# Mirrored positions and 64x64 quadrants in the Fourier part of a fused S4 and PEER kernel

## The chip, the cores and the metric

The kernel runs on one core of one Trainium2 chip. The metric is the device time of one execution in microseconds; three runs of the kernel before gave a median of 1520.82 us (1519.2 to 1524.14).

## The reference

Two branches read the same input `u` (2048 positions, 576 channels) and are mixed by a gate.

```python
# branch A: a long convolution over positions, one kernel K per channel
P = jnp.exp(logdA[:, :, None] * l[None, None, :])
K = jnp.einsum("dn,dnl,dn->dl", Cc, P, dB).real
Kf, Uf = rfft(pad(K)), rfft(pad(u))
y = irfft(Uf * Kf)[:L] + u * Dskip
# branch B: PEER, per token and head the best 2 of 64 x 64 experts by two score tables
s1 = jnp.einsum("nhd,ed->nhe", q1, k1); s2 = jnp.einsum("nhd,ed->nhe", q2, k2)
# top_s, top_e: the best 2 of the 2 x 2 candidates of the two top-2 lists
g = softmax(top_s)
act = gelu(jnp.einsum("nd,nhkd->nhk", x, u[top_e]))
b = jnp.einsum("nhk,nhk,nhkd->nd", g, act, v[top_e])
# mix
gate = sigmoid((x * gate_w).sum(-1))
return gate * a + (1 - gate) * b
```

## The kernel before, in words

Five engines work on one program whose order was fixed when it was written out: Python generators (one per piece of work) run on a model of the engines' clocks, `pump` lets those go on whose inputs the model holds to be ready, and so their instructions come to stand between others. `mm` (line 202 in the profile holds every matmul) and the `Engine` wrapper (line 122: every DVE, ACT and POOL operation) keep that clock; `dma` (line 193) issues nearly all transfers on SP's queue. `quota`, `need`, `take` and `free` count PSUM banks (`sc` for scores, activations and outputs, `wb` for the rest) and buffers.

**PEER.** 128 groups of score matmuls (`s`, 14 matmuls 128x128x512 in fp16, one group per 8 score tables and 128 tokens), each followed on DVE by eight MAX8 and eight FIND_INDEX8 (`scores_top`). 128 groups of activation matmuls (`a`, 14 matmuls as well: all 4096 experts against all tokens), whose results go to DRAM by way of `go`. The main loop (lines 1495 to 1533) takes a group of the one or the other kind and calls `pump` between its matmuls. The list `acts` (line 1437) holds the order of the activation groups; its last 20 are those of expert block 7 with block 6's last one between. The output loop (line 1543) takes 16 tiles of 128 tokens: `prep(t)` loads the activations of tile t, builds one-hot matrices on DVE, scatters the gate weights by matmul (`S`), multiplies and splits them (`wh`), and 192 matmuls 128x128x288 (`o`) sum over the experts.

**The convolution.** The length-2048 transform is split into 32 x 64: stage 1 transforms over the 32 positions l1 of one residue l2 (64 residues), stage 2 over the 64 residues.
- `k_gen` makes K: 36 chunks of 16 channels, in fp32 matmuls 128x32x64 (`kb`); `k_store` splits a chunk into two fp16 parts in `ko` (two buffers) and stores it to `k_d`.
- `u_stage1` and `k_stage1` multiply by constant tables (`tu`, `tk`; fp16 in two parts) and store to `su_d` and `sk_d`, rows of residue, part (real, imaginary) and frequency k1. `k_stage1` has, for each of 32 pairs of residues, eight matmuls of 144 columns.
- `products` (line 1014): for each of 16 values of k and each third of the channels (192 columns), one fp32 product with the 128x128 matrix `f2` for u (`pu`) and one for K (`pk`), both with 2 x 192 columns. The matrix is the complex 64-point transform written out in real and imaginary parts. ACT copies the results into four tiles (`vf`, `ux`, `kr`, `kx`) such that real parts and imaginary parts stand where the complex multiplication wants them; POOL does two multiplications and an addition; the product with `fi` (`pv`) transforms back. It is sent out by `back` together with the forward products of three steps later. `store` copies it to `vo` and `z_d`.
- `y_part` does the inverse of stage 1, two output tiles at a time: fp32 products 128x64x288 with `tf` (`y`), scaled and added to `u * Dskip`. It runs inside the output loop: `load` asks for the next pair's data when the last pair is finished.

The stages follow one another in `freq`: load `ksb` (all of `k_d`), `k_stage1`, `products`, then the values' preparation and `prep(0)`.

Of the kernel before, what the change touches and what calls it, by code (L numbers as in the profile page):

```python
# [35 lines left out]
L2_POS = list(range(32)) + [63 - i for i in range(32)]  # L36
KB = 4
# [5 lines left out]
def _tables():  # L43
# [7 lines left out]
    def stacked(rows, inner):  # L51

        x = np.zeros((len(rows), 2, R1, 2, R1, 2))
        for b in range(2):
            x[:, b, :, b] = fwd[rows[:, b]]
        if inner:
            x = x.transpose(0, 1, 2, 5, 4, 3)
        else:
            x = x.transpose(0, 2, 1, 3, 5, 4)
        x = (x * 2.0 ** 14).reshape(len(rows), 64, 128)  # L60
        hi = x.astype(np.float16)
        lo = (x - hi).astype(np.float16)
        x = np.stack([np.concatenate([hi, hi], 1), np.concatenate([lo, np.zeros_like(lo)], 1)], 2)
        return np.ascontiguousarray(x.transpose(1, 0, 2, 3))

    tu = stacked(np.arange(R2).reshape(32, 2), False)
    tk = stacked(np.array(L2_POS)[:, None].repeat(2, 1), True)
    tf = np.zeros((NT, 2, 2, R1, 2, 2, R1))
    for t in range(NT):
        for pr in range(2):  # L70
            for b in range(2):
                w = 4 * t + 2 * pr + b
                tf[t, pr, b, :, :, b] = inv[w].transpose(1, 2, 0)
    tf = tf.transpose(0, 1, 2, 4, 3, 5, 6).reshape(NT * 2, 128, 64).transpose(1, 0, 2)
    k2 = np.arange(R2)
    al = 2 * np.pi * (np.outer(l2, k2) % R2) / R2
    c, s = np.cos(al), np.sin(al)
    f2 = np.zeros((R2, 2, 2, R2))
    f2[:, 0, 0], f2[:, 1, 0] = c, s
    f2[:, 0, 1], f2[:, 1, 1] = -s, c  # L80
    fi = np.zeros((2, R2, R2, 2))
    fi[0, :, :, 0], fi[1, :, :, 0] = c.T, -s.T
    fi[0, :, :, 1], fi[1, :, :, 1] = s.T, c.T
# [43 lines left out]
def body(ctx: ExitStack, tc: tile.TileContext, xT, au, par, logdt, dskip, gatew, wq, kT, uT, vv,  # L127
# [148 lines left out]
    quota(sc=4, wb=0, kb=4, hw=1, slot=9, go=3, m8=2, raw=1, ko=2)  # L276
# [8 lines left out]
    su_d = dr.tile([R2, 2, R1, D], F32, name="su_d")  # L285
    sk_d = dr.tile([R2, 2, R1, D], F32, name="sk_d")
    k_d = dr.tile([NCK, 128, 2, R2 * NI], F16, name="k_d")
    z_d = dr.tile([R2, 2, R1, D], F32, name="z_d")
# [12 lines left out]
    def au_load(a, t):  # L301
        for d, o in au_rows(au, t, a):
            dma(o, d)

# [467 lines left out]

    def k_store(c, kb):
# [5 lines left out]
        kz = ko.rearrange("p z (q i) -> p z q i", i=NI)  # L779
# [7 lines left out]
        kstored[0] += 1  # L787
# [135 lines left out]
    def u_stage1():  # L923
# [7 lines left out]
        def half(m):  # L931
            for n in range(m, 2 * NT, 2):
                a, o = us[:, m, :], us[:, 2 + m, :]
                for z in range(2):
                    dma(a[64 * z:64 * z + 64], bass.AP(tensor=au.tensor, offset=au.offset + 2 * n * D,
                                                       ap=[[64 * D, R1], [D, 2], [1, D]]))
# [8 lines left out]
                for hh in range(2):  # L945
# [6 lines left out]
                    ov = o.rearrange("p (b j q) -> p j b q", b=2, j=2)[:, hh]  # L952
                    S.activation(ov, pb[:, :288].rearrange("p (b q) -> p b q", b=2), AF.Copy)
# [3 lines left out]
                dma(su_d[2 * n:2 * n + 2].rearrange("b r k d -> (b r k) d"), o)  # L957
# [14 lines left out]
    def k_stage1(ksb, fk):  # L972
        enter, leave, count = ring(3)

        def tail(w, o, pbs):
            yield from ready(*pbs)
            for z in range(2):
                copy(o[:, z if w < 32 else 1 - z, :], pbs[z][:, :288])
                free("wb", o)
            yield from ready(o)  # L980
            l0 = min(L2_POS[w], L2_POS[w + 1])
            dma(bass.AP(tensor=sk_d.tensor, offset=sk_d.offset + l0 * R1 * 2 * D,
                        ap=[[288, 128], [R1 * 2 * D, 2], [1, 288]]), o)
# [7 lines left out]
        nxt = load(0)  # L991
        for w0 in range(0, 64, 16):
            tkt = nxt
            if w0 < 48:
                nxt = load(w0 + 16)
            yield from ready(tkt, ksb)
            for w in range(w0, w0 + 16, 2):
                yield from enter()
                o = fk.tile([128, 2, 288], F32, tag="s1o", name=f"k1o{w}", bufs=4)
                pbs = []  # L1000
                yield from need("wb", 2)
                for z in range(2):
                    pb = bank("wb", f"k1_{w}_{z}")
                    for jp in range(2):
                        for n in range(2):
                            mm(pb[:, 144 * jp:144 * jp + 144], tkt[:, w + z - w0, n], ksb[:, jp, :, w + z, :],
                               n == 0, n == 1)
                    pbs.append(pb)
                spawn(tail(w, o, pbs))
                del pb, pbs  # L1010
# [3 lines left out]
    def products(ff):  # L1014
# [11 lines left out]
        top, low = slice(0, 64), slice(64, 128)  # L1026
        made = []

        def tail(nm, pu, pk, v):

            t = lambda g: ff.tile([128, 2, PW], F32, tag=g, name=g + nm, bufs=2)
            ux, kr, ki = t("ux"), t("kr"), t("kx")
            two = lambda x: x[:, 0:2 * PW].rearrange("p (z q) -> p z q", z=2)
            yield from ready(pu)
            S.activation(v, two(pu), AF.Copy)
            S.activation(ux[top], two(pu)[low], AF.Copy)
            S.activation(ux[low], two(pu)[top], AF.Copy)
            free("wb", ux)
            yield from ready(pk)
            S.activation(kr[top], two(pk)[top], AF.Copy)  # L1040
            S.activation(kr[low], two(pk)[top], AF.Copy)
            S.activation(ki[top], two(pk)[low], AF.Copy, scale=-1.0)
            S.activation(ki[low], two(pk)[low], AF.Copy)
            free("wb", ki)
            yield from ready(v, ux, kr, ki)
# [6 lines left out]
        def store(k, hh, vo, pv):  # L1052
            yield from ready(pv)
            copy(vo[:, :, PW * hh:PW * hh + PW], pv[:, 0:2 * PW].rearrange("p (z q) -> p z q", z=2))
            free("wb", vo)
# [5 lines left out]
        def back(nm, k, hh, v, vo):  # L1061
            pv = bank("wb", f"pv_{nm}")
            mm(pv[:, 0:2 * PW], fi, v.rearrange("p z q -> p (z q)"), True, True)
            spawn(store(k, hh, vo, pv))
# [3 lines left out]
        for k in range(16):  # L1068
# [7 lines left out]
            for hh in range(3):  # L1076
# [6 lines left out]
                yield from need("wb", 3 if last else 2)  # L1083
                nm = f"{k}_{hh}"
                both = []
# [8 lines left out]
                spawn(tail(nm, *both, v))  # L1094
                del pb, both
        for last in queue:
# [3 lines left out]
            yield from need("wb")  # L1100
# [4 lines left out]
    def freq():  # L1105
# [4 lines left out]
        ksb = KS.__enter__().tile([128, 2, NCK, R2, NI], F16, name="ksb")  # L1110
        for n in range(2):
            half = slice(NCK // 2 * n, NCK // 2 * (n + 1))
            for jp in range(2):
                for z in range(2):
                    while wire[0] > clock[0] + 2:
                        yield 0.3
                    dma(ksb[64 * z:64 * z + 64, jp, half].rearrange("p c q i -> p c (q i)"),
                        k_d[half, 64 * jp:64 * jp + 64, z].rearrange("c p n -> p c n"))
# [179 lines left out]
    def prep(t):  # L1298
# [6 lines left out]
        while len(placed) <= t:  # L1305
# [31 lines left out]
        if t + 1 < NT:  # L1337
            spawn(prep(t + 1))
# [5 lines left out]
        for q in range(4):  # L1344
            bs = slice(8 * q, 8 * q + 8)
            src = gl[q // 2][:, 8 * (q % 2):8 * (q % 2) + 8]
            if t < 2 and V.free > clock[0] + 6 and max(G.free, S.free) < clock[0] + 1:
# [13 lines left out]
    def y_part():  # L1361

        def load(t):
            a = oy.tile([128, D], F32, tag="ya", name=f"ya{t}", bufs=4)
            au_load(a, t)
            z = oy.tile([128, 2, D], F32, tag="yz", name=f"yz{t}", bufs=2)
            dma(z, z_d[4 * t:4 * t + 4].rearrange("(p b) r k d -> (b r k) p d", b=2))
            tf = oy.tile([128, 2, 64], F32, tag="tf", name=f"tf{t}", bufs=2)
            dma(tf, tf_d[:, 2 * t:2 * t + 2, :])
            return a, z, tf  # L1370

        db = row(dskip, "db", oy)
        nxt = load(0), load(1)
# [242 lines left out]
```

## Time and profile before

| | us |
|---|---|
| median of three runs | 1520.82 |
| profiled execution, first to last instruction (span) | 1519.4 |
| TensorE busy (PE) | 1484.3 |
| VectorE busy (DVE) | 1227.3 |
| ScalarE busy (ACT) | 884.0 |
| GpSimd busy (POOL) | 533.0 |
| TensorE weight loads (PEld, beside PE) | 899.0 |

PE is matmuls, PEld weight loads. A fp32 matmul leaves two records. In the rows of groups and tiles, `pu<-ui,cst` means that `pu` is written from `ui` and `cst`; `x96` is the number of records. In a timeline row the columns are start, length to the end of the last record (with the drain of the array, which overlaps the next matmul), engine, line, operation and count. In the table of stages each engine's busy time stands with its count of instructions, then the granted TensorE clock, the DMA engines' share and GB/s.

### The profile page before, as it was taken

What the parts mean: (1) busy time and instruction counts of PE and PEld (TensorE: products, weight loads), DVE (VectorE), ACT (ScalarE), POOL (GpSimd) and SP (SyncE); (2) the same over time, 40 slices, a digit from 0 to 9 for tenths busy, and PEclk for the clock granted to TensorE, in tenths of its full rate; (3) what the DMA queues carried; (4) which work ended last, traced back from release to release, by engine and by line L of the source; (5) the groups of instructions that cost most, each with busy time, mean ns of one, the idle gap of its engine ahead of it and who ended that gap; (6) DMA issues with size and microseconds to landing.
All of it is one profiled execution on the core that took longest, in us unless ns stands there. A gap on an engine that the chain in (4) does not pass through costs nothing. (4 is left out here: it accounts for less than half of the span.)

```text
span 1519.4 us, 35924 instructions
## 1 busy us (share of the span) xinstructions
PE 1484.3 (98%) x13410; PEld 899.0 (59%) x13414; DVE 1227.3 (81%) x4583; ACT 884.0 (58%) x1456; POOL 533.0 (35%) x528
## 2 busy tenths in 40 slices
PE   6999999999999999999999999999999999999999
PEld 3445554454455545555555455545787888888887
DVE  5988999889987997678885665549999898898860
ACT  5557868678768677225689999956242332332320
POOL 0454656363644653002447898521100000000100
PEclk9999999999999999999999999999999999999999
DMA  6343452353435324976645558476732442432400
GB/s 224 126 127 124 135 157 74 119 178 94 130 123 147 107 76 145 187 213 240 241 157 197 186 182 274 136 243 203 231 118 92 141 131 85 142 124 92 142 17 17
DMA packets 154031, 223.26 MB, mean 147 GB/s; under 512 B 11904, under 2 KB 105984, under 8 KB 147200
## 3 DMA queue, kind: packets, MB, share of 16 engines
q1 hardware_dynamic: 153760, 220.88, 46.4%
q8 instruction: 106, 1.74, 0.5%
q14 instruction: 69, 0.57, 0.1%
q10 hardware_dynamic: 96, 0.07, 0.0%
HBM read 149.60 MB, written 71.30 MB: 145 GB/s over the span
## 5 line engine op out<-in xcount | busy, mean ns | idle before, releaser
L202 PE MATMUL o<-vhl,wh 128*128 128x288 f16 x3072 | 387.3, 286 | 0.0
L202 PE MATMUL s<-whl,xb 128*128 128x512 f16 x1536 | 369.4, 381 | 6.1 <-DVE whl L122 2.5
L202 PE MATMUL a<-xb,uhl 128*128 128x512 f16 x1536 | 365.4, 381 | 3.1 <-DVE i L122 3.1
L202 PEld LDWEIGHTS <-wh 128*128 128x128 f16 x3072 | 295.9, 98 | 76.2 <-issue 3.5
L202 PEld LDWEIGHTS <-xb 128*128 128x128 f16 x1792 | 173.3, 98 | 209.2 <-issue 15.7
L202 PEld LDWEIGHTS <-uhl 128*128 128x128 f16 x1536 | 148.9, 99 | 177.6 <-issue 6.0
L122 DVE FIND_INDEX8 i<-m,s 128x8 uint32<-128x64 f32 x1024 | 206.4, 222 | 0.0
L122 ACT ACTIVATE wh<-gl,s_wg 128x1024 f16<-128x1024 f32 x64 | 68.8, 1138 | 209.9 <-DVE gl L122 209.9
L122 DVE MAX8 m<-s 128x8 f32<-128x64 f32 x1024 | 146.3, 214 | 37.6 <-PE s L202 37.1
L122 POOL TENSOR_TENSOR CS<-CS,ex 128x512 f32<-128x512 f32 x72 | 99.9, 1419 | 179.3 <-DVE ex L122 167.0
L122 POOL TENSOR_TENSOR ya<-ya,db 128x576 f32<-128x576 f32 x16 | 29.4, 1838 | 338.2 <-DVE Bg L122 195.5
L122 ACT ACTIVATE go<-a,i_a 128x512 f32<-128x512 f32 x90 | 61.6, 686 | 77.3 <-PE a L202 47.3
L122 DVE TENSOR_TENSOR gl<-S,gl 128x256 f32<-128x256 f32 x256 | 90.0, 415 | 9.5 <-PE S L202 7.1
L122 DVE SCALAR_TENSOR_TENSOR wh<-gl,s_wg,wh 128x1024 f16<-128x1024 f32 x64 | 87.9, 1405 | 11.3 <-ACT wh L122 11.3
L122 POOL TENSOR_TENSOR e<-aN,rt 128x512 f32<-128x512 f32 x72 | 82.4, 1163 | 28.4 <-PE kb L202 28.4
L122 ACT ACTIVATE gl<-gl 128x1024 f32<-128x1024 f32 x64 | 63.5, 1045 | 41.6 <-DMA gl<-g_d 41.5
L122 DVE TENSOR_TENSOR Bg<-Be,vals 128x1024 f16<-128x1024 f16 x128 | 84.0, 698 | 2.2
L122 DVE TENSOR_TENSOR A<-iota_a,vals 128x2048 f16<-128x2048 f16 x64 | 84.4, 1319 | 0.0
L202 PE MATMUL s<-wrem,xb 128*128 128x512 f16 x256 | 76.2, 379 | 0.4 <-DVE xb L122 0.4
L202 PE MATMUL a<-xb,wrem 128*128 128x512 f16 x256 | 76.6, 381 | 0.0
L202 PEld LDWEIGHTS <-A 128*128 128x128 f16 x2048 | 70.7, 97 | 6.5 <-issue 1.2
L202 PE MATMUL S<-Bg,A 128*128 128x64 f16 x2048 | 73.0, 193 | 1.6 <-DVE Bg L122 1.5
(202 smaller groups left out, 2326.7 us busy)
## 6 DMA issues: line engine op xcount, KB each, us to landing
g_d<-go SPq DMA_DIRECT2D x128, 256.0 KB, 2.5
gl<-g_d SPq DMA_DIRECT2D x32, 1024.0 KB, 5.6
wq<-in_wq_dram SPq DMA_DIRECT2D x16, 1152.0 KB, 6.4
us<-in_au_dram SPq DMA_DIRECT2D x64, 144.0 KB, 3.0
su_d<-us SPq DMA_DIRECT2D x32, 288.0 KB, 2.1
sk_d<-k1o SPq DMA_DIRECT2D x32, 288.0 KB, 3.7
vn<-in_vv_dram SPq DMA_DIRECT2D x32, 288.0 KB, 3.5
ui<-su_d SPq DMA_DIRECT2D x16, 576.0 KB, 4.0
```

The costliest lines, as they stand in the source:

```text
L122: return f(*a, **k)
L202: T.matmul(o, l, r, start=start, stop=stop)
```

## The change

- **Stage 1.** Instead of one transform per residue l2, a pair of mirrored residues (l and 64 - l for u; w and 63 - w for K) goes through one table, which gives sums and differences: four real rows per frequency (`U_PAIRS`, `stacked`). `su_d`, `sk_d` and `z_d` get four planes of 32 residues. `pair_rows` addresses one pair in all four planes.
- **Stage 2.** On sums and differences the 64-point transform falls into real 64x64 matrices, four in `f2` and four in `fi`. In `products` each 128x128 product becomes four products 64x64x192, each in one quadrant of the array (`quads`: rows 0 to 63 or 64 to 127 of the input, partitions 0 to 63 or 64 to 127 of the output). Real parts go to one PSUM bank (`pr`), imaginary parts to another (`pi`), of u and K side by side, so that two copies replace the seven; POOL multiplies twice and adds and subtracts halves. The backward product fills two banks, each copied by itself.
- **Inverse of stage 1.** One table of a pair serves two mirrored output tiles, so `y_part` works on tiles p and 15 - p. `ORDER` is the order of the output loop, and `acts` puts tokens' block 3 of expert block 7 ahead of blocks 1 and 2. The products are 128x32x288.
- **K to stage 1.** Chunks are stored in twos (`k_d` has 18 places, `ko` one buffer of twice the size), and `ksb` holds the mirrored residues on the partitions. `k_stage1` has four matmuls of 288 columns per pair of residues.

```diff
+U_PAIRS = [(0, 32)] + [(n, 64 - n) for n in range(1, 32)]
+ORDER = [t for p in range(8) for t in (p, 15 - p)]
...
-    quota(sc=4, wb=0, kb=4, hw=1, slot=9, go=3, m8=2, raw=1, ko=2)
+    quota(sc=4, wb=0, kb=4, hw=1, slot=9, go=3, m8=2, raw=1, ko=1)
...
+    def pair_rows(x, n):
+
+        return bass.AP(tensor=x.tensor, offset=x.offset + n * R1 * D, ap=[[D, R1], [32 * R1 * D, 4], [1, D]])
...
     def k_store(c, kb):
         yield from ready(kb)
-        yield from need("ko")
-        take("ko", "ko")
-        ko = kg.tile([128, 2, NI * R2], F16, tag="ko", name=f"ko{c}", bufs=2)
+        if c % 2 == 0:
+            yield from need("ko")
+            take("ko", "ko")
+            kos[c // 2] = kg.tile([128, 2, 2 * NI * R2], F16, name="ko", tag="ko", bufs=1)
+        while c // 2 not in kos:
+            yield 0.2
+        ko = kos[c // 2]
...
-        dma(k_d[c], ko)
+        kstored[0] += 1
+        kos[c // 2, c % 2] = 1
+        if (c // 2, 1 - c % 2) not in kos:
+            return
+        dma(k_d[c // 2].rearrange("p z m q -> p z (m q)"), ko)
...
+            for hh in range(2):
+                pb = bank("wb", f"k1_{w}_{hh}")
+                for n in range(2):
+                    mm(pb[:, :288], tkt[:, w % 16, n], ksb[:, 2 * hh:2 * hh + 2, :, w, :].rearrange("p j c i -> p (j c) i"),
+                       n == 0, n == 1)
...
+        quads = [(slice(0, 64), slice(0, 64)), (slice(0, 64), slice(64, 128)),
+                 (slice(64, 128), slice(0, 64)), (slice(64, 128), slice(64, 128))]
+
+        def tail(nm, pbs, v):
+
+            t = ff.tile([128, 2, 2, PW], F32, tag="tt", name="tt" + nm, bufs=2)
+            for n, p in enumerate(pbs):
+                yield from ready(p)
+                copy(t[:, n].rearrange("p u q -> p (u q)"), p[:, 0:2 * PW])
+                free("wb", t)
+            yield from ready(t)
+            u = t[:, :, 0, :]
+            k = [t[:, n:n + 1, 1, :].to_broadcast([128, 2, PW]) for n in range(2)]
             M = V if max(V.free, clock[0]) < max(G.free, clock[0]) - 2.5 else G
-            M.tensor_mul(v, v, kr)
-            M.tensor_mul(ux, ux, ki)
-            G.tensor_add(v, v, ux)
+            M.tensor_mul(v, u, k[0])
+            M.tensor_mul(u, u, k[1])
+            G.tensor_sub(v[:, 0], v[:, 0], t[:, 1, 0, :])
+            G.tensor_add(v[:, 1], v[:, 1], t[:, 0, 0, :])
...
+            for n, pv in enumerate(pvs):
+                copy(vo[:, n, PW * hh:PW * hh + PW], pv[:, 0:PW])
+                free("wb", vo)
...
-            mm(pv[:, 0:2 * PW], fi, v.rearrange("p z q -> p (z q)"), True, True)
+            pvs = [bank("wb", f"pv_{nm}_{n}") for n in range(2)]
+            for n, (rows, cols) in enumerate(quads):
+                mm(pvs[n // 2][cols, 0:PW], fi[rows, cols], v[rows, n % 2, :], True, True, 0.085)
...
-                yield from need("wb", 3 if last else 2)
+                yield from need("wb", 4 if last else 2)
                 nm = f"{k}_{hh}"
-                for x, q in ((ui, "pu"), (ki, "pk")):
-                    pb = bank("wb", q + nm)
-                    mm(pb[:, 0:2 * PW], f2, x[:, :, cs], True, True)
-                    both.append(pb)
+                both = [bank("wb", q + nm) for q in ("pr", "pi")]
+                for z, x in enumerate((ui, ki)):
+                    for n, (rows, cols) in enumerate(quads):
+                        mm(both[n // 2][cols, PW * z:PW * z + PW], f2[rows, 64 * z:64 * z + 64], x[rows, n % 2, cs],
+                           True, True, 0.085)
...
-            z = oy.tile([128, 2, D], F32, tag="yz", name=f"yz{t}", bufs=2)
-            dma(z, z_d[4 * t:4 * t + 4].rearrange("(p b) r k d -> (b r k) p d", b=2))
+            z = oy.tile([128, 4, D], F32, tag="yz", name=f"yz{p}", bufs=1)
+            for j in range(4):
+                dma(z[:, j], pair_rows(z_d, 4 * p + j))
...
-                    for pr in range(2):
-                        mm(pb[64 * pr:64 * pr + 64, :288], tf[:, pr, :], z[:, pr, 288 * hh:288 * hh + 288], True, True, 0.27)
+                    for j in range(4):
+                        w = 3 - j if n else j
+                        mm(pb[32 * j:32 * j + 32, :288], tf[:, w, 32 * n:32 * n + 32], z[:, w, 288 * hh:288 * hh + 288],
+                           True, True, 0.13)
...
-    acts = [(c, tb, j) for c, tb in [(c, tb) for c in range(7) for tb in range(4 if c < 6 else 3)] + [(7, 0), (6, 3), (7, 1), (7, 2), (7, 3)]
+    acts = [(c, tb, j) for c, tb in [(c, tb) for c in range(7) for tb in range(4 if c < 6 else 3)] + [(7, 0), (6, 3), (7, 3), (7, 1), (7, 2)]
```

More of the change, by code (lines that the diff above doesn't have):

```diff
@@ L49, in _tables, with stacked @@
     inv = np.stack([np.cos(th), -np.sin(th)], -1) / L
[L51 to L60, printed above, removed]
+    def stacked(pairs):
+        x = np.zeros((len(pairs), 2, R1, R1, 4))
+        for n, (l, m) in enumerate(pairs):
+            if l + m == R2 // 2:
+                x[n, 0, :, :, 0], x[n, 0, :, :, 2] = fwd[l, ..., 0], fwd[l, ..., 1]
+                x[n, 1, :, :, 1], x[n, 1, :, :, 3] = fwd[m, ..., 0], fwd[m, ..., 1]
+                continue
+            for b, (w, sign) in enumerate(((l, 1), (m, -1))):
+                re, im = fwd[w, ..., 0], fwd[w, ..., 1]
+                x[n, b] = np.stack([re, sign * im, im, sign * re], -1)
+        x = (x.transpose(0, 2, 1, 3, 4) * 2.0 ** 14).reshape(len(pairs), 64, 128)
@@ new lines, in stacked @@
+        return x.transpose(1, 2, 0, 3, 4)
+    tu = np.ascontiguousarray(stacked(U_PAIRS).reshape(128, 32, 2, 128))
+    tk = stacked([(w, 63 - w) for w in range(32)]).reshape(2, R1, 2, 32, 2, 128).swapaxes(0, 1)
+    tk = np.ascontiguousarray(tk.reshape(128, 32, 2, 128))
+    tf = np.zeros((32, R1, 4, 2, R1))
+    for w in range(32):
+        for b, sign in enumerate((-1, 1)):
+            re, im = inv[63 - w if b else w].transpose(2, 1, 0)
+            tf[w, :, 0, b], tf[w, :, 2, b] = re, im
+            tf[w, :, 1, b], tf[w, :, 3, b] = sign * im, sign * re
@@ new lines, in _tables, with mirror @@
+    tf = tf.reshape(32, 128, 64).transpose(1, 0, 2)
+    k2 = np.arange(R2)
+    def mirror(d, sign):
+        al = 2 * np.pi * np.outer(d, k2) / R2
+        return np.concatenate([np.cos(al), sign * np.sin(al)], 0)
+    du, dk = np.arange(32.0), 31.5 - np.arange(32)
+    f2 = np.zeros((2, R2, 2, R2))
+    for g, sign in enumerate((1, -1)):
+        f2[g, :, 0] = mirror(du, sign)
+        f2[g, 32, 0] = (-1.0) ** k2
+        f2[g, :, 1] = mirror(-dk, sign)
+    fi = np.zeros((2, R2, 2, R2))
+    fi[:, :, 0] = mirror(dk, 1).T
@@ L284, in body @@
     g_d = dr.tile([NT, 128, 32, 128], F32, name="g_d")
[L285 to L288, printed above, removed]
+    su_d = dr.tile([4, 32, R1, D], F32, name="su_d")
+    sk_d = dr.tile([4, 32, R1, D], F32, name="sk_d")
+    k_d = dr.tile([NCK // 2, 128, 2, 2, R2 * NI], F16, name="k_d")
+    z_d = dr.tile([4, 32, R1, D], F32, name="z_d")
     def row(x, name, pool):
@@ L976, in tail @@
             yield from ready(*pbs)
-            for z in range(2):
-                copy(o[:, z if w < 32 else 1 - z, :], pbs[z][:, :288])
+            for hh in range(2):
+                copy(o[:, 288 * hh:288 * hh + 288], pbs[hh][:, :288])
                 free("wb", o)
             yield from ready(o)
-            l0 = min(L2_POS[w], L2_POS[w + 1])
-            dma(bass.AP(tensor=sk_d.tensor, offset=sk_d.offset + l0 * R1 * 2 * D,
-                        ap=[[288, 128], [R1 * 2 * D, 2], [1, 288]]), o)
+            dma(pair_rows(sk_d, w), o)
             leave(w)
@@ L989, in load @@
             return tkt
[L991 to L995, printed above, removed]
-            yield from ready(tkt, ksb)
[L997 to L1010, printed above, removed]
+        tabs = load(0), load(16)
+        for w in range(32):
+            tkt = tabs[w // 16]
+            yield from ready(tkt, ksb)
+            yield from enter()
+            o = fk.tile([128, D], F32, tag="s1o", name=f"k1o{w}", bufs=4)
+            pbs = []
+            yield from need("wb", 2)
+            for hh in range(2):
+                pb = bank("wb", f"k1_{w}_{hh}")
+                for n in range(2):
+                    mm(pb[:, :288], tkt[:, w % 16, n], ksb[:, 2 * hh:2 * hh + 2, :, w, :].rearrange("p j c i -> p (j c) i"),
+                       n == 0, n == 1)
+                pbs.append(pb)
+            spawn(tail(w, o, pbs))
+            del pb, pbs
         while count() < 32:
@@ L1025, in products, with store @@
         parts = {}
-        top, low = slice(0, 64), slice(64, 128)
         made = []
[L1029 to L1045, printed above, removed]
+        quads = [(slice(0, 64), slice(0, 64)), (slice(0, 64), slice(64, 128)),
[9 more added lines that the diff above has]
+            k = [t[:, n:n + 1, 1, :].to_broadcast([128, 2, PW]) for n in range(2)]
             M = V if max(V.free, clock[0]) < max(G.free, clock[0]) - 2.5 else G
-            M.tensor_mul(v, v, kr)
-            M.tensor_mul(ux, ux, ki)
-            G.tensor_add(v, v, ux)
+            M.tensor_mul(v, u, k[0])
+            M.tensor_mul(u, u, k[1])
+            G.tensor_sub(v[:, 0], v[:, 0], t[:, 1, 0, :])
+            G.tensor_add(v[:, 1], v[:, 1], t[:, 0, 0, :])
             made.append(nm)
[L1052 to L1055, printed above, removed]
+        def store(k, hh, vo, pvs):
+            yield from ready(*pvs)
+            for n, pv in enumerate(pvs):
+                copy(vo[:, n, PW * hh:PW * hh + PW], pv[:, 0:PW])
+                free("wb", vo)
             yield from ready(vo)
@@ L1109, in freq @@
         V.memset(wrems[3][64:128, 1, :], 0.0)
[L1110 to L1118, printed above, removed]
+        ksb = KS.__enter__().tile([128, 4, NCK // 2, 32, 2 * NI], F16, name="ksb")
+        for j in range(4):
+            while wire[0] > clock[0] + 2:
+                yield 0.3
+            dma(ksb[:, j].rearrange("p c w i -> p c (w i)"),
+                k_d[:, 32 * j:32 * j + 32].rearrange("c l z m n -> (l z m) c n"))
         fk = FK.__enter__()
@@ L1304, in prep @@
             dma(gl[h], g_d[t][:, 16 * h:16 * h + 16])
-        while len(placed) <= t:
+        while t not in placed:
             yield 0.3
@@ L1346, in prep @@
             src = gl[q // 2][:, 8 * (q % 2):8 * (q % 2) + 8]
-            if t < 2 and V.free > clock[0] + 6 and max(G.free, S.free) < clock[0] + 1:
+            if t in ORDER[:2] and V.free > clock[0] + 6 and max(G.free, S.free) < clock[0] + 1:
                 S.activation(fl(h[0][:, bs]), fl(src), AF.Copy, scale=s_wg)
@@ L1361, in y_part, with load @@
     def y_part():
-        def load(t):
-            a = oy.tile([128, D], F32, tag="ya", name=f"ya{t}", bufs=4)
-            au_load(a, t)
-            z = oy.tile([128, 2, D], F32, tag="yz", name=f"yz{t}", bufs=2)
-            dma(z, z_d[4 * t:4 * t + 4].rearrange("(p b) r k d -> (b r k) p d", b=2))
-            tf = oy.tile([128, 2, 64], F32, tag="tf", name=f"tf{t}", bufs=2)
-            dma(tf, tf_d[:, 2 * t:2 * t + 2, :])
-            return a, z, tf
-        db = row(dskip, "db", oy)
-        nxt = load(0), load(1)
-        for t in range(0, NT, 2):
-            two = nxt
-            yield from ready(*[x for y in two for x in y], late=4.0)
-            for a, z, tf in two:
+        def load(p):
+            ya = []
+            for t in ORDER[2 * p:2 * p + 2]:
+                a = oy.tile([128, D], F32, tag="ya", name=f"ya{t}", bufs=4)
+                au_load(a, t)
+                ya.append(a)
+            z = oy.tile([128, 4, D], F32, tag="yz", name=f"yz{p}", bufs=1)
+            for j in range(4):
+                dma(z[:, j], pair_rows(z_d, 4 * p + j))
+            tf = oy.tile([128, 4, 64], F32, tag="tf", name=f"tf{p}", bufs=1)
+            dma(tf, tf_d[:, 4 * p:4 * p + 4, :])
+            return ya, z, tf
+        db = row(dskip, "db", oy)
+        nxt = load(0)
+        for p in range(NT // 2):
+            ya, z, tf = nxt
+            yield from ready(*ya, z, tf, late=4.0)
+            for a in ya:
                 G.tensor_mul(a, a, db)
-            while t >= 2 and t - 2 not in finished:
+            while p and ORDER[2 * p - 2] not in finished:
                 yield 0.5
@@ L1529, in body @@
                     adone[0] += 1
-                    if c == 7:
-                        free("slot")
+                if not acts:
+                    free("slot")
                 continue
@@ L1542, in body @@
     spawn(y_part())
-    for t in range(NT):
+    for t in ORDER:
         until(lambda: t in st)
```

79 lines of the change are left out of this document (31 added, 48 removed).

## The prediction

> **What bounds the kernel now.** I read the page's busy line first, then busy time by stage, then TensorE's timeline inside the stages that the change touches.
>
> ```profile
> span 1519.4 us, 35924 instructions
> PE 1484.3 (98%) x13410; PEld 899.0 (59%) x13414; DVE 1227.3 (81%) x4583; ACT 884.0 (58%) x1456; POOL 533.0 (35%) x528
> ```
>
> ```profile
> core 0: us, PE busy (x) PEld busy (x) DVE busy (x) ACT busy (x) POOL busy (x), PEclk, DMA share, GB/s
> 0.00:621.00 621.00, 600.43 (x5641) 305.86 (x5646) 536.76 (x2148) 432.90 (x631) 295.69 (x242) 0.99 0.43 131
> 621.00:663.00 42.00, 42.00 (x338) 21.87 (x337) 39.02 (x318) 7.51 (x13) 0.81 (x3) 1.00 0.96 192
> 663.00:744.00 81.00, 76.56 (x669) 45.54 (x667) 65.56 (x488) 38.73 (x112) 15.44 (x52) 1.00 0.73 245
> 744.00:1001.00 257.00, 252.22 (x1259) 129.88 (x1258) 162.61 (x969) 234.34 (x516) 181.37 (x209) 1.00 0.55 185
> 1001.00:1063.00 62.00, 62.00 (x455) 31.23 (x453) 51.77 (x71) 39.10 (x52) 10.32 (x6) 1.00 0.76 254
> 1063.00:1520.00 457.00, 451.14 (x5058) 364.61 (x5056) 371.59 (x594) 131.38 (x133) 29.41 (x16) 1.00 0.35 111
> ```
>
> The rows are: generating the convolution kernel (to 621 us), loading `ksb`, stage 1 of that kernel (663 to 744), the products stage (744 to 1001), the rest of the PEER scores and activations, and the output loop. TensorE is the full engine in every one of them: it lacks 20.6 us in the first row and 15 us in all the others. The freq work is no phase of its own for TensorE: `pump` slips it between score (`s`) and activation (`a`) matmuls, which always have something to run. So a microsecond less of TensorE work anywhere before the output loop should be a microsecond less of time, as long as nothing else starts to make it wait. In the products stage ACT is at 234.34 of 257 us, POOL at 181.37.
>
> **The products stage (the main term).** One step (16 values of k x 3 column thirds = 48) looks like this on TensorE:
>
> ```profile
> 880.41 0.81 PE L202 MATMUL pu<-ui,cst 128*128 128x384 f32 x2
> 881.05 0.81 PE L202 MATMUL pk<-ki,cst 128*128 128x384 f32 x2
> 881.70 0.81 PE L202 MATMUL pv<-vf,cst 128*128 128x384 f32 x2
> 882.34 1.46 PE L202 MATMUL s<-whl,xb 128*128 128x512 f16 x6
> 883.64 0.59 PE L202 MATMUL s<-wrem,xb 128*128 128x512 f16 x2
> ```
>
> The second column includes the drain; the starts count: 882.34 - 880.41 = 1.93 us for three fp32 products, 0.643 each, so 0.322 per record (each product leaves two) and 0.84 ns per column and record. The change turns each 128x128x384 product into four 64x64x192 ones, each in its own quadrant of the array. Two forward products become eight, the backward one four: 12 products, 24 records of 192 columns. A record's stream is 192 x 0.84 = 0.161 us, and everything hangs on how many run at once. No 64-row tile stands in this trace, but column tiles do:
>
> ```profile
> 151.68 0.29 PE L202 MATMUL kb<-Y,CS 128*32 128x64 f32 x8
> 151.79 0.29 PE L202 MATMUL kb<-e,CS 128*32 128x64 f32 x8
> 151.91 0.29 PE L202 MATMUL kb<-Y,CS 128*32 128x64 f32 x8
> 152.02 0.29 PE L202 MATMUL kb<-e,CS 128*32 128x64 f32 x8
> ```
>
> Eight records of 64 columns, rotating through four column tiles, start every 0.113 us. One stream is 64 x 0.84 = 0.054, so eight fill two rounds of 0.0565: four run at once, fp32, four different moving operands, with 3 ns of overhead per round. I take the same for the four quadrants: six rounds of 0.161 + 0.002 = 0.163, 0.978 us a step. The bounds from rows are this, and nothing at once (24 x 0.161 = 3.86); I take the near end because the nearest row is a four-tile row with the same element type, and the edit sends the two row halves to different PSUM banks.
>
> Entering and leaving a tiled mode costs. The trace shows it around `y` (two 64-column tiles):
>
> ```profile
> 1076.78 1.02 PE L202 MATMUL o<-vhl,wh 128*128 128x288 f16 x7
> 1077.73 2.16 PE L202 MATMUL y<-yz,tf 128*64 128x288 f32 x16
> 1079.82 2.38 PE L202 MATMUL o<-vhl,wh 128*128 128x288 f16 x18
> ...
> 1139.76 4.33 PE L202 MATMUL o<-vhl,wh 128*128 128x288 f16 x34
> 1143.93 0.19 PE L202 MATMUL S<-Bg,A 128*128 128x64 f16 x1
> ```
>
> 34 `o` records take 4.17 us, 0.1226 each. From 1076.78 to 1079.82 are 3.04 us; less 7 x 0.1226 = 0.86 and less eight rounds of 288 x 0.84 = 0.242 (1.94), 0.24 to 0.25 us is left for both switches. Before, the products ran in the mode of their neighbours and paid nothing. After, each visit pays 0.25 (below nothing is excluded: nothing is switched today).
>
> A full step: 0.98 + 0.25 = 1.23 instead of 1.93: -0.70 us. 45 steps do forward and backward in one visit: -31.5. The first three have no backward part: 4 x 0.163 + 0.25 = 0.90 instead of 1.29, -1.2. Three last backward visits: 0.33 + 0.25 = 0.58 instead of 0.64, -0.2. **Sum -32.9 us.**
>
> **What follows the products.** The evictions:
>
> ```profile
> L122 ACT ACTIVATE vf<-pu x48: 469/491/635, 745.1 to 991.5; 128x384 f32<-128x384 f32 x48
> L122 ACT ACTIVATE ux<-pu x96: 482/486/490, 745.6 to 992.5; 64x384 f32<-64x384 f32 x96
> L122 ACT ACTIVATE kr<-pk x96: 468/483/485, 746.6 to 993.5; 64x384 f32<-64x384 f32 x96
> L122 ACT ACTIVATE kx<-pk x96: 485/487/488, 747.6 to 994.5; 64x384 f32<-64x384 f32 x96
> L122 DVE COPY vo<-pv x38: 531/557/559, 757.0 to 991.8; 128x384 f32<-128x384 f32 x38
> L122 POOL TENSOR_TENSOR vf<-vf,kr x47: 991/997/1074, 747.7 to 994.1; 128x384 f32<-128x384 f32 x47
> L122 DVE COPY k1o<-k 128x288 f32<-128x288 f32 x12 | 5.2, 454 | 11.4 <-PE k L202 5.2 <-ACT k1o L122 4.2 <-PE s L202 1.2
> L122 POOL TENSOR_TENSOR ggd<-ggd,i_x 128x64 f32<-128x64 f32 x8 | 2.3, 292 | 0.6
> ```
>
> Before, one step costs ACT 0.49 + 2 x 0.486 + 2 x 0.483 + 2 x 0.487 = 3.40 us, and one 384-wide `vo` copy (0.557 on DVE). After: two 384-wide copies (0.49 or 0.557) and two 192-wide ones, each under the 0.454 of 288 columns: 2.0 us at most, spread by `copy` over ACT and DVE. ACT loses at least 48 x 1.4 = 67 of its 234 us. POOL: before 3 x 0.997 = 2.99; after two 384-wide and two 192-wide, these between 0.292 (64 wide) and 0.997, by their slope 0.57: 3.13. Nothing here is TensorE time; what becomes late next is POOL: 181.37 + 48 x 0.14 = 188 us of a stage that should shrink to about 224. It fits.
>
> Banks get tighter: a step now wants four free of the five, before three, and each is back only when its copy is done.
>
> **Stage 1 of the kernel.**
>
> ```profile
> 710.96 0.67 PE L202 MATMUL k<-ksb,tk 128*128 128x144 f16 x8
> 711.47 0.81 PE L202 MATMUL s<-whl,xb 128*128 128x512 f16 x3
> ```
>
> Eight records of 144 columns in 0.51 us, 64 ns each, 256 of them 16.3 us. After: 128 of 288 columns at 0.1226, 15.7. **-0.6 us.** Two 288-wide copies and one store per pair as before.
>
> **Edits that I cost at nothing.** `y`: 16 products of 288 columns per pair in four 32-column tiles instead of eight in two 64-column tiles: 32 records four at a time are the same eight rounds and the same two switches. Its `z` loads become four issues per pair for two, its `tf` loads one for two, all asked for a pair ahead; the output loop covers them. Were that cover gone, one issue's 0.39 us of SP (below) would show eight times. Stage 1 of `u` has the same matmuls and copies, other rows. `ksb` comes in 4 transfers for 8 with the same bytes, under `s` matmuls. The added wait: an even chunk's `ko` copy, on ACT, must wait for the pair's store, since there is one buffer. Behind it on ACT stand the exponentials of the next chunks and `go` evictions.
>
> ```profile
> L193 SPq DMA_DIRECT2D k_d<-ko x36: 319/344/1698, 156.6 to 616.0; - x36
> L193 SPq DMA_DIRECT2D yz<-z_d x16: 388/389/1410, 1068.8 to 1420.0; - x16
> ```
>
> Stores come every (616.0 - 156.6) / 35 = 13 us, so a pair has 26 us to leave: no wait.
>
> The order of output tiles (0, 15, 1, 14, ...) needs activations of block 3 early; `acts` is reordered for it:
>
> ```profile
> 999.35 0.81 PE L202 MATMUL pv<-vf,cst 128*128 128x384 f32 x2
> ...
> 1023.74 1.13 PE L202 MATMUL S<-Bg,A 128*128 128x64 f16 x32
> ...
> 1059.54 1.13 PE L202 MATMUL S<-Bg,A 128*128 128x64 f16 x32
> ...
> 1062.77 0.59 PE L202 MATMUL a<-xb,wrem 128*128 128x512 f16 x2
> 1063.20 2.98 PE L202 MATMUL o<-vhl,wh 128*128 128x288 f16 x23
> ```
>
> Tile 0's `S` starts at 1023.74, the second tile's at 1059.54, the last activation ends at 1063.2. The second tile now needs block 3, whose last group stands 8 groups before the end (a group has 14 records of 512 columns; six take 883.64 - 882.34 = 1.30 us, so 8 x 14 x 0.217 = 24 us), so at about 1039 on this clock: 20 us before it is used. Nothing.
>
> **The sum** is -32.9 - 0.6 = -33.5 us. On the profiled span 1519.4 that is 1485.9; the median of the three runs is 1520.82, 1.4 above, so 1487.3. I say **1487**. Its own range is 1478 to 1495: downward the stalls of 663 to 1001 (4.4 + 4.8 us) may go with ACT's load, upward a reshuffled order may cost as much.
>
> **Rivals.**
> 1. *The row halves do not overlap* (the change doesn't do what it says). Column tiles are shown at once; 64-row tiles nowhere. If the upper and the lower half take turns, a round is 0.326: 6 x 0.326 + 0.25 = 2.21 per step, +0.28 x 45 = +12.6, the six outer visits +1.6, stage 1 -0.6: **1534, slower**. It decides from a round above (1.93 - 0.25) / 6 = 0.28 us. Against it: `kb`. Chance 0.09.
> 2. *Three at a time in effect.* A round of 4/3 x 0.163 = 0.217: 1.55 per step, -0.38 x 45 = -17.1, -0.4 outside, -0.6: **1503**. The page "TensorE: Matmul & The Clock Gate" of the Trainium skill, Part 3, gives four row tiles 3.07 times one; an estimate by that page is a round of 0.21 and 1502. The `kb` rows show the full four for column tiles, so chance 0.05.
> 3. *The products stage keeps its pace.* If POOL, or the wish for four of five banks, holds it to 257 us, it still ends near 1000 while the activations, 33 us shorter, end near 1030. Tile 0's `S` came 24 us after the last `pv`, then 40 us to the first `o`, of which at least half is `S` and its followers: `o` starts near 1045, 15 us of TensorE are idle: **1502**. For it: POOL is at 71% already. Against: ACT (91%) was the full one and is relieved. Chance 0.06. The page "TensorEngine Tiling (Array Packing)" of the Trainium skill, section Performance Considerations, speaks for this one: tiling speeds TensorE and not the emptying of PSUM, which may become the bottleneck. By that rule alone the time is this rival's; the rows of the copies (3.96 us a step before, at most 2.0 after) bear it out little here.
> 4. *Small new stalls eat it all*: 1517 to 1524. Chance 0.04.
>
> The forecast itself has 0.76. Measurement of this kernel tells about 0.3%, 4.6 us, from no change. Faster: 0.76 + 0.05 + 0.06 = 0.87; same 0.04; slower 0.09. The range takes in the forecast and rivals 2 and 3: 1477 to 1506, leaving out rivals 1 and 4 and some edges.
>
> **What would show it.** In the profile after: a visit of 24 records after which the next `s` starts about 1.2 us after its first; `a` ending near 1030; the output loop of unchanged length (457 us); ACT in the products stage under 75% and POOL over 80%. A span between two rounds of `pr`/`pi` of 0.32 instead of 0.16 would prove rival 1; TensorE idle between the last `a` and the first `o`, rival 3.

## The result and the profile after

The kernel after takes 1483.01 us (median of four runs, 1480.29 to 1486.46) beside 1520.32 us before: a ratio of 0.9755, 95% interval 0.9735 to 0.9776, or 37.3 us less. The forecast was 1487. The profiled execution has a span of 1481.5 us (1519.4 before).

The page's first lines of the kernel after:

```profile
span 1481.5 us, 37353 instructions
PE 1449.1 (98%) x14274; PEld 875.7 (59%) x14278; DVE 1232.2 (83%) x4601; ACT 772.3 (52%) x1267; POOL 537.2 (36%) x562
```

TensorE's busy time fell by 35.2 us, its idle time by 2.7 (35.1 to 32.4); together the 37.9 us of the two spans. ACT lost 112 us, and TensorE is at 98% as before: the kernel is bound by the same engine, with less on it.

Busy time of the kernel after in the same stretches of time as before (columns as there):

```profile
0.00:621.00 621.00, 603.52 (x5628) 306.79 (x5634) 539.74 (x2156) 426.96 (x621) 296.06 (x245) 0.99 0.44 135
621.00:663.00 42.00, 42.00 (x329) 22.73 (x326) 29.65 (x213) 13.76 (x26) 2.73 (x9) 1.00 0.66 231
663.00:744.00 81.00, 79.57 (x654) 44.19 (x653) 71.16 (x530) 42.97 (x127) 18.09 (x56) 1.00 0.67 222
744.00:1001.00 257.00, 254.02 (x2360) 128.59 (x2358) 198.71 (x1089) 137.84 (x335) 176.06 (x230) 0.99 0.62 204
1001.00:1063.00 62.00, 55.61 (x586) 38.96 (x585) 57.03 (x81) 29.75 (x38) 20.77 (x12) 0.94 0.73 250
```

Up to 744 us TensorE now lacks 18.9 us, before 25.0. Of these 6 us, 3 lie between 663 and 744 us (4.4 to 1.4), where the prediction's range allowed for it; 3 lie before 621 us, which no step of it named. From 1001 to 1063 it lacks 6.4 where it lacked nothing, at a granted clock of 0.94: a new stall.

One step of the products stage on TensorE, kernel after:

```profile
799.32 1.46 PE L213 MATMUL s<-whl,xb 128*128 128x512 f16 x6
800.71 0.38 PE L213 MATMUL pr<-ui,cst 64*64 64x192 f32 x2
800.72 0.38 PE L213 MATMUL pi<-ui,cst 64*64 64x192 f32 x2
800.92 0.33 PE L213 MATMUL pr<-ui,cst 64*64 64x192 f32 x2
...
801.25 0.33 PE L213 MATMUL pr<-ki,cst 64*64 64x192 f32 x2
801.26 0.33 PE L213 MATMUL pi<-ki,cst 64*64 64x192 f32 x2
801.41 0.51 PE L213 MATMUL pv<-vf,cst 64*64 64x192 f32 x8
801.85 0.60 PE L213 MATMUL s<-whl,xb 128*128 128x512 f16 x2
```

Two `pr` and two `pi` records start within 0.02 us, the next four 0.16 to 0.21 us later: all four quadrants run at once, upper and lower rows too. From the first product to the next `s` are 1.14 us. Six `s` records end their turn at 799.32 + 6 x 0.217 = 800.62, so 0.09 us went into the switch ahead: 1.23 us a step, as worked out. Before it was 1.93.

The start of the output loop, TensorE, then ACT and DVE of the kernel after:

```profile
1015.61 2.10 PE L213 MATMUL S<-Bg,A 128*128 128x64 f16 x64
1017.54 2.37 PE L213 MATMUL o<-vhl,wh 128*128 128x288 f16 x18
1024.19 0.24 PE L213 MATMUL S<-Bg,A 128*128 128x64 f16 x1 [4.28 <-DVE Bg L133]
1024.79 1.81 PE L213 MATMUL S<-Bg,A 128*128 128x64 f16 x31 [0.36 <-DVE Bg L133]
1026.41 5.44 PE L213 MATMUL o<-vhl,wh 128*128 128x288 f16 x30
```

```profile
1007.33 8.32 ACT L133 ACTIVATE vhl<-vhl,sci 128x576 f16<-128x576 f32 x12
1015.55 3.99 ACT L133 ACTIVATE gl<-gl 128x1024 f32<-128x1024 f32 x4
```

```profile
1012.69 0.75 DVE L133 TENSOR_SCALAR go<-a,i_a 128x512 f32<-128x512 f32 x1 [2.73 <-DMA g_d<-go]
1013.36 4.33 DVE L133 SCALAR_TENSOR_TENSOR vhl<-vhl,sci,vhl 128x576 f16<-128x576 f32 x3
1018.31 0.75 DVE L133 TENSOR_SCALAR go<-a,i_a 128x512 f32<-128x512 f32 x1 [0.62 <-DMA g_d<-go]
1018.98 0.41 DVE L133 TENSOR_TENSOR gl<-S,gl 128x256 f32<-128x256 f32 x1
...
1022.48 2.25 DVE L133 TENSOR_TENSOR Bg<-Be,vals 128x1024 f16<-128x1024 f16 x2
```

The first `o` comes 45.7 us earlier than before (1017.54 for 1063.20), but the loop to the end takes 464.0 us for 456.2. TensorE's busy time up to the first `o`, in the view of stretches:

```profile
0.00:1017.54 1017.54, 995.65 (x9090) 510.80 (x9095) 852.70 (x4000) 633.73 (x1126) 499.89 (x543) 0.99 0.52 167
```

Before, the same view has 1033.4 us busy of 1063.2. So the 45.7 us are 37.8 of work and 7.9 of idle time; in the loop TensorE is then busy 2.5 us longer (453.5 for 450.9) and idle 5.2 us longer. Profiles of one kernel differ here: the kernel after taken again has its first `o` at 1020.7 and 997.5 us busy, and `e_lean` and `e_order` below, which have the 8354 matmul records of the kernel before up to there, are busy 1028.9 and 1030.2 us. A shift of the first `o` by 3 us, or of the work by 4, therefore tells nothing by itself.

Read the chain backward: the second tile's third quarter of `S` waits 4.28 us for one-hot matrices (`Bg`), which DVE made only after multiplying `gl` (1018.98). Two things were late ahead of that multiplication. ACT's gelu of `gl` stood behind twelve copies of the values (`vhl`), 8.3 us in a row, and ended at 1019.54. DVE itself waited 2.73 us and 0.62 us for stores of activations (`g_d<-go`) to give back their buffers, with 4.33 us of the values' work between; it stood idle only 0.24 us between the first `gl` and the next three. Behind the wait thirty `o` take 5.28 us (1026.41 to 1031.69, where the next `S` starts) instead of 3.68, at a granted clock of 0.69 between 1026 and 1032 us.

### The profile page after: what moved, and what is told of

It is laid out like the page before. It is cut to its first block, busy times and chain, and to the rows that moved or that the text cites. A ratio compares the mean times of both kernels' runs of the same rounds, so it can differ in the third digit from the quotient of the medians.

```text
span 1481.5 us, 37353 instructions
## 1 busy us (share of the span) xinstructions
PE 1449.1 (98%) x14274; PEld 875.7 (59%) x14278; DVE 1232.2 (83%) x4601; ACT 772.3 (52%) x1267; POOL 537.2 (36%) x562
## 4 chain that ended last, share of the span: by engine, by line
PE 83%; DVE 7%; DMA 5%; ACT 3%; issue 1%; SPq 0%; ACTq 0%; DVEq 0%
PE o L213 24%; PE s L213 22%; PE a L213 20%; PE S L213 4%; PE wb L213 2%; PE pr L213 2%; PE kb L213 2%; DMA ur<-in_uT_dram 1%; PE y L213 1%; PE pv L213 1%; DVE i L133 1%; PE kP L213 1%; PE u L213 1%; DMA g_d<-go 1%; PE k L213 1%
## 5 line engine op out<-in xcount | busy, mean ns | idle before, releaser
L133 DVE TENSOR_TENSOR Bg<-Be,vals 128x1024 f16<-128x1024 f16 x128 | 90.6, 749 | 2.2
L133 DVE TENSOR_TENSOR A<-iota_a,vals 128x2048 f16<-128x2048 f16 x64 | 77.7, 1214 | 0.0
```

The costliest lines, as they stand in the source:

```text
L133: return f(*a, **k)
```

## The experiments

Theory A: the kernel's time is TensorE's, and the quadrants gave what they took off it; ACT's relief only lets the stage follow. Theory B: the relief of ACT itself is the gain. Times are medians; ratios are to the kernel before on the same chip.

**Every quadrant product twice** (`e_twice`).

```diff
-                for z, x in enumerate((ui, ki)):
+                for z, x in ((0, ui), (1, ki), (0, ui), (1, ki)):
-            for n, (rows, cols) in enumerate(quads):
+            for n, (rows, cols) in list(enumerate(quads)) * 2:
```

> The kernel after with every quadrant product of the products stage issued twice (the second writes the same result over the first). Theory A (TensorE is full everywhere, so its time in the products stage is the kernel's time, one for one): a full step gains six rounds of 0.163 = 0.98 us, 45 of them, the outer visits 3 x 0.65 + 3 x 0.33, together +47 us, 1530 us. Theory B (the gain came from the copies that ACT lost, TensorE would have had room): at most +10, 1493 us.

1517.21 us, ratio 0.9979 (0.9965 to 0.9992): +34 on the kernel after. The first `o`:

```profile
1059.46 1.13 PE L213 MATMUL S<-Bg,A 128*128 128x64 f16 x32
1060.43 1.75 PE L213 MATMUL o<-vhl,wh 128*128 128x288 f16 x13
```

Up to there the extra work costs 1060.43 - 1017.54 = 42.9 of the 47 us (39.7 against the kernel after taken again), nearly one for one. Then the output loop takes 1515.4 - 1060.4 = 455 us instead of 464: the new stall is gone when the activations end late. The time lies between the 1530 us of theory A and the 1493 of theory B. Theory B is out as the whole story, and the end of the kernel is not TensorE's sum alone.

**Four copies put back on ACT** (`e_copies`), ahead of the step's own:

```diff
...
                 yield from ready(p)
+                for z in range(2):
+                    hz = slice(64 * z, 64 * z + 64)
+                    S.activation(junk[hz], p[hz, 0:2 * PW], AF.Copy)
                 copy(t[:, n].rearrange("p u q -> p (u q)"), p[:, 0:2 * PW])
```

> The kernel after with four copies of 64 partitions x 384 put back on ACT in each step, ahead of the two that it has, into a tile that nothing reads: 48 x 4 x 0.486 = 93 us of ACT's work back, in the place where it was. Theory A: ACT is at 138 of 257 us in the products stage, so the copies fit beside; 1483 to 1488 us. Theory B: the kernel loses what the copies had given, at least half of the 37 us, 1501 us or more.

1499.99 us, ratio 0.9857 (0.9838 to 0.9876): +17, near theory B's bound and not the 1483 to 1488 of theory A, with not a matmul more (ACT's busy time rose by 65 us to 837.8; `copy` sent other copies to DVE). The last backward product comes at 984.9 us (933.9 in the kernel after), by the rows of the tile `pv`:

```profile
L213 PE MATMUL pv<-vf,cst x384: 322/323/577, 749.1 to 984.9; 64*64 64x192 f32 x192
```

TensorE's timeline has tile 0's `S` and the first `o`:

```profile
1003.96 1.13 PE L213 MATMUL S<-Bg,A 128*128 128x64 f16 x32
...
1025.31 0.65 PE L213 MATMUL o<-vhl,wh 128*128 128x288 f16 x4
```

And the stretch behind it, in the view of busy time by stretches:

```profile
1025.00:1128.00 103.00, 92.22 (x1095) 72.87 (x1093) 94.09 (x140) 43.95 (x50) 18.68 (x12) 0.98 0.49 161
```

Tile 0's `S` starts at 1004.0 instead of 976.6, since `prep(0)` follows the products stage; the first `o` is 7.8 us later, and from there to the end the kernel takes 471.4 us instead of 464.0, with TensorE lacking 10.8 of the 103 us from 1025. This is the condition of rival 3 of the prediction (a products stage that ends late, 1502 us). The time is near, the place of the loss is not: rival 3 wanted 15 us of idle TensorE between the last `a` and the first `o`, and here the `o` follow the last `a` at once and the idle time comes behind.

**The same copies behind POOL's work** (`e_later2`): the edit stands after `made.append(nm)` and reads `v`.

> The kernel after with four 64x384 copies more on ACT in each step, as in the run with copies ahead, but behind POOL's four operations of the step: they read the product in SBUF, and no bank waits for them. If ACT's load is what cost 17 us there: 1498 to 1502 us again. If it was the copies' place ahead of the step's own two (banks, then POOL, then the stage's end come later): 1483 to 1488 us.

1496.11 us, ratio 0.9843 (0.9821 to 0.9865): +13. Most of the cost is ACT's load, a lesser part (4 us) may be the place. The same edit with copies that read `t` gave no time: its instructions waited for one another without end.

```profile
1021.16 3.84 PE L213 MATMUL o<-vhl,wh 128*128 128x288 f16 x30
1036.00 0.23 PE L213 MATMUL S<-Bg,A 128*128 128x64 f16 x1 [11.01 <-DVE Bg L133]
```

Here the first `o` is 3.6 us late, hardly more than two profiles of the kernel after differ, and one wait of 11.01 us follows: the loss sits at the start of the output loop.

**ACT's relief alone** (`e_lean`), in the kernel before:

```diff
-            S.activation(ux[top], two(pu)[low], AF.Copy)
-            S.activation(ux[low], two(pu)[top], AF.Copy)
+            S.activation(ux, two(pu), AF.Copy)
...
-            S.activation(kr[top], two(pk)[top], AF.Copy)
-            S.activation(kr[low], two(pk)[top], AF.Copy)
-            S.activation(ki[top], two(pk)[low], AF.Copy, scale=-1.0)
-            S.activation(ki[low], two(pk)[low], AF.Copy)
+            S.activation(kr, two(pk), AF.Copy)
+            S.activation(ki, two(pk), AF.Copy)
```

> The kernel before with four full copies on ACT in each products step instead of seven (real and imaginary halves are not exchanged and no sign is changed, so this leaves out part of the computation): ACT loses 48 x 1.44 = 69 us in the products stage, as it does with the change, and TensorE's work stays. Theory A (TensorE's time alone sets the end; ACT's relief is only what lets the stage follow): 1515 to 1521 us. Theory B (ACT's relief is worth something by itself): 1510 us or less.

1520.31 us, ratio 0.9996 (0.9984 to 1.0008): nothing. The products stage in the view of stretches:

```profile
744.00:1001.00 257.00, 257.00 (x1300) 133.53 (x1299) 163.22 (x952) 152.49 (x382) 179.27 (x205) 1.00 0.57 189
```

The first `o` on TensorE's timeline, and the wait behind it:

```profile
1053.45 2.37 PE L202 MATMUL o<-vhl,wh 128*128 128x288 f16 x18
1060.60 0.20 PE L202 MATMUL S<-Bg,A 128*128 128x64 f16 x1 [4.78 <-DVE Bg L122]
```

TensorE lacks nothing in the products stage (4.8 us before) and reaches the output loop 9.8 us earlier than in the kernel before, 5.2 of them idle time and the rest shorter busy time for the same records; the loop gives it all back, 8.9 us of it in waits for `Bg`. Ahead of the longest of them (4.78 us) DVE waited 2.5 and 2.8 us for stores of `go`. So B is out: the relief is worth nothing by itself, and 13 to 17 us together with the quadrants. One thing moved with the edit: the matmul behind the values' scale (`pvn`, the end of `v_norm`) starts at 972.1 us here, at 935.6 in the kernel before. So what the relief would be worth with that in its place is not shown; in the products stage it could not exceed the 4.8 us that TensorE lacked there.

**Two more changes of tiling per step** (`e_switch`):

```diff
                 if last:
+                    mm(both[1][:, 400:401], identb, onesb[:, 0:1], True, True, 0.1)
                     back(*last)
```

> The kernel after with one 128x128 bf16 product of one column put between the forward and the backward products of a step, into an unused column of the bank of imaginary parts: two more changes of tiling in 45 steps. Theory A: a pair of changes costs 0.25 us as around y, 45 x 0.25 = +11 us and 1 us for the products, 1495 us. Rival: a change costs only where the array would have drained anyway, the 0.25 is the ends of long matmuls; +2 us, 1485 us.

1490.94 us, ratio 0.9796 (0.9772 to 0.9820): +8.

```profile
801.01 0.38 PE L213 MATMUL pr<-ui,cst 64*64 64x192 f32 x2
...
801.83 0.18 PE L213 MATMUL pi<-onesb,identb 128*128 128x1 bf16 x1
801.93 0.56 PE L213 MATMUL pv<-vf,cst 64*64 64x192 f32 x8
802.42 0.60 PE L213 MATMUL s<-wrem,xb 128*128 128x512 f16 x2
```

A step is 1.41 us instead of 1.14: 0.27 for a pair of changes with the small product, the price of theory A. 45 of them are 12 us; 8 arrive, by the same give and take at the output loop (the first `o` at 1031.6 us, 14.1 later, and a loop of 459.0).

**The order of the quadrants** (`e_halves`: both upper ones for u and K, then both lower ones; `e_tile`: u and K of one quadrant, then the next).

> The kernel after with the forward products in another order: first the two of the upper rows for u and for K, then the two of the lower rows for u and for K; the same eight products. If four products run at once only because four neighbours in the program lie in four quadrants (theory C), two run at once here: eight rounds of 0.163 for four, +0.65 us in each of 48 steps, +31 us, 1514 us. If the array takes what it can from further back in its queue (theory D), nothing changes: 1483 us.

> The kernel after with the forward products ordered by quadrant: u and K of the first, then of the second, third and fourth; the same eight products. With the upper and lower rows swapped in blocks the time had stayed, since the lower rows' products began before the upper rows' were through. If column tiles get past each other in the same way, nothing changes: 1483 us. If only the row halves have queues of their own, two products run at once (one of each half): eight rounds of 0.163 us for four, +0.65 us x 48 = +31 us, 1514 us.

1482.80 us (ratio 0.9732, 0.9707 to 0.9757) and 1482.35 us (0.9761, 0.9737 to 0.9784): no change. In `e_halves` the program has `pr<-ui`, `pr<-ki`, `pi<-ui`, `pi<-ki`; the array ran:

```profile
800.04 0.38 PE L213 MATMUL pr<-ui,cst 64*64 64x192 f32 x2
800.06 0.38 PE L213 MATMUL pi<-ui,cst 64*64 64x192 f32 x2
800.25 0.33 PE L213 MATMUL pr<-ui,cst 64*64 64x192 f32 x2
800.28 0.33 PE L213 MATMUL pi<-ui,cst 64*64 64x192 f32 x2
800.41 0.33 PE L213 MATMUL pr<-ki,cst 64*64 64x192 f32 x2
```

The lower rows' first product (`pi<-ui`) starts 0.35 us before the upper rows' product with K (`pr<-ki`), which is written ahead of it. That the written order reached the engine is to be seen in the starts: the first `pi` starts 13 to 14 ns after the first `pr` in the kernel after, where two products are written ahead of it, and 26 to 27 ns in `e_halves` and `e_tile`, where four are (in 46 of 47 steps of each trace).

**The new order of output tiles alone** (`e_order`), in the kernel before: `ORDER`, the changed `acts` and what follows from them in `prep`, `y_part` and the output loop.

> The kernel before with the changed order of output tiles (0, 15, 1, 14, ...) and of the activation groups, and nothing else. If the new stall at the start of the output loop (about 8 us against the kernel before) comes from the order, since the second tile now waits for token block 3: +5 to +8 us, 1526 to 1529 us. If it comes from the activations ending 46 us earlier while the values' preparation is where it was: 1520 us, no change.

1520.56 us, ratio 1.0008 (0.9993 to 1.0022): the order is not what stalls the output loop.

**The values' scale earlier** (`e_norm`, and again beside the kernel after):

```diff
-            yield 2
+            yield 0.5
```

> The kernel after with a pause of 0.5 instead of 2 model microseconds between the 48 rows of v_norm, so that the scale of the values is known earlier than at 935 us and their splitting on ACT and DVE leaves the start of the output loop and gives its buffer back sooner. If that preparation is what stands in the way there: 1475 to 1478 us. If the second tile waits for its activations and for DVE's own one-hot work: 1483 us, no change.

> The kernel after with the shorter pause in v_norm, again, beside the kernel after. Its output loop was 9 us shorter but began 7 us later. If the end is set by what the second and third tiles' preparation needs, both ways end at one time: within 2 us of the kernel after. If the stall removed is a gain: 2 to 5 us less.

> The kernel after, unchanged, on the same chip as the next one: 1483 us, as the comparison for it.

1480.14 us (ratio 0.9740, 0.9712 to 0.9769), and taken again 1481.47 (1479.22 to 1484.21) beside 1483.78 for the kernel after (1481.46 to 1486.89). The stretch from 1001 to 1063 us in `e_norm`:

```profile
1001.00:1063.00 62.00, 60.83 (x648) 41.23 (x644) 56.73 (x93) 24.77 (x27) 7.00 (x4) 1.00 0.64 205
```

Its first `o`:

```profile
1024.61 5.55 PE L213 MATMUL o<-vhl,wh 128*128 128x288 f16 x44
```

`pvn` starts at 889.3 us for 940.4 in the kernel after, and the values' last copies on ACT at 989.2 for 1022.7. The stall is gone (1.2 us lacking for 6.4, full clock), so the values' preparation was in the way; DVE's waits for stores of `go` are gone with it (none from 995 to 1035 us), and no run separates the two. The loop begins 7 us later, 3.4 between the two taken side by side (1024.1 for 1020.7): 64 more records of `S` now stand ahead of the first `o` (256 for 192; 32 take 0.97 us, so 1.9 us), and the rest is within what two profiles of one kernel differ. The time lies between the two that were expected, and the 2 to 3 us between the medians are inside the spread of the runs: no version here is clearly better than the kernel after.

## Why the prediction was right, point by point

- *TensorE is full, so its saved time is the kernel's.* Right up to the output loop (`e_twice`: 42.9 of 47 us arrive), and incomplete after it: time won or lost ahead of the loop is partly given back at its start (34 of 47 us arrive, 8 of 12, and none of the 9.8 by which `e_lean` is early).
- *Four quadrants at once; a step 1.23 us for 1.93.* Right: 1.14 us and 0.09 us for the switch ahead; a doubled step of `e_twice` takes 2.11 us (871.93 to 874.04), 0.97 more for six more rounds. The column tiles of `kb` were a sound witness for row tiles. *Rival 1* (halves take turns) and *rival 2* (three at once) are out by the same rows. The Trainium skill's page "TensorE: Matmul & The Clock Gate", Part 3, gives 3.07 times for four row tiles; the four quadrants of this stream do better, and the measured step decides: 1.23 us, and not the 1.55 of rival 2.
- *0.25 us for both changes of tiling.* Right: 0.27 with the small product.
- *Stage 1, `y`.* Right, from rows of the kernel after:

```profile
704.69 0.65 PE L213 MATMUL k<-ksb,tk 128*128 128x288 f16 x4
705.17 1.46 PE L213 MATMUL s<-whl,xb 128*128 128x512 f16 x6
...
1040.10 2.15 PE L213 MATMUL y<-yz,tf 128*32 128x288 f32 x32
1042.17 1.03 PE L213 MATMUL o<-vhl,wh 128*128 128x288 f16 x7
```

Four `k` records in 0.48 us (eight took 0.51), a visit of `y` 2.07 us (2.09).
- *ACT under 75%, POOL over 80% of the products stage.* Right: of the 175 us from 739 to 914 ACT had 85.49, 49%, and POOL 145.62, 83%. That the stage would shrink to about 224 us was wrong: its products run from 739.7 to 933.9 us, 744.3 to 999.4 before, so it lost 61 us where the prediction took 33 off TensorE's work in it. Its pace before was thus not TensorE's but in good part ACT's, which was at 91%: with ACT's relief alone (`e_lean`) the products take 218 us (742.3 to 960.3) instead of 255, and with copies put back (`e_copies`) 245 instead of 194. The row of 739 to 914:

```profile
739.00:914.00 175.00, 172.73 (x1716) 88.21 (x1715) 144.18 (x983) 85.49 (x241) 145.62 (x192) 0.99 0.63 210
```

- *The order of tiles costs nothing.* Right (`e_order`).
- *The activations end near 1030, and the output loop keeps its 457 us.* Both wrong, in opposite directions: the last `a` started at 1015.4 and the first `o` came at 1017.5, the loop took 464. Ahead of the loop 6 us of idle time vanished before 744 us. All profiles of the kernel after and its variants lack 18 to 21 us there, the kernel before, `e_lean` and `e_order` 24 to 25; so neither the order of tiles nor ACT's relief did it, and which edit did is open. At the loop, the step that failed is the unchanged 457 us: it puts at nothing that the loop comes earlier and the values' preparation does not. The prediction asked when the second tile's activations are ready and found 20 us to spare. But the values' scale, set by `v_norm`, had not come earlier (`pvn` at 940.4 us for 935.6), so ACT's gelu stood behind the values' copies, and DVE's multiplication behind their other half and two waits for stores. The runs agree: where `pvn` stands 91 to 135 us ahead of the first `o`, the loop takes 455 to 459 us (the kernel before, `e_order`, `e_twice`, `e_switch`, `e_norm`); where it stands 77 and 81 us ahead, 464 and 466 (the kernel after, `e_lean`). Only `e_copies` and `e_later2`, with more copies on ACT, take longer than that, at 119 and 92 us. Which of the waits counted is open.
- *Rival 3* did not happen, since ACT was relieved. `e_copies` makes its condition, at 1500 us for the 1502 worked out, though the idle time falls in another place, so that the near number is in part luck. The fewer copies were no side effect of the change but a condition for a third to a half of its gain (13 to 17 of 37 us). The Trainium skill's page "TensorEngine Tiling (Array Packing)", section Performance Considerations, says that the emptying of PSUM may become the bottleneck once TensorE is tiled. This case agrees in part: with four more copies out of PSUM 17 of 37 us are lost, but 13 of them also with copies that read SBUF (`e_later2`), so most of it is the load on the engine that empties PSUM.
- The sum, -33.5 for -37.3, is 4 us short. Its term for the work is borne out as far as profiles agree: up to the first `o` TensorE is busy 31 to 38 us less (995.7 and 997.5 us in two profiles of the kernel after; 1033.4, 1030.2 and 1028.9 in the kernel before and its two variants with the same records). The idle time that vanished ahead of the loop (7.9 us) and the longer loop (7.8) are no terms of the sum and happen to cancel: that it comes so near is in that part luck.

## What to carry to other kernels

When one engine is full everywhere, price a change by that engine's rows and look for the nearest tiled row as a witness of concurrency; here it gave the step of 1.23 us as measured. Then ask what the saved time runs into: the next stage's preparation has its own start, and work that ends earlier than that preparation turns into waiting (the output loop grew from 456 to 464 us). And where a change relieves two engines, test each alone: here one relief was worth 0 by itself, and without it the other lost 13 to 17 of 37 us.

## What the runs showed of the hardware

Products in different quadrants pass each other: written as upper, upper, lower, lower they start as upper, lower, upper, lower (800.04, 800.06, 800.41), and even u and K of one quadrant written next to each other cost nothing (1482.35 us). So it was the set of quadrants in a stretch of the program that counted, not their order, at least within eight products.
